# Window attention, then top-1 MoE: column groups for small last blocks, experts 1 and 2 swapped, one pass of 160 columns, held products at the end, maxima scaled by ScalarE

## The chip, the cores and the metric

The kernel runs on one core of one Trainium2 chip. The metric is the device time of one execution in microseconds (us), and less is better. TensorE (PE) does the matrix products, VectorE (DVE), ScalarE (ACT) and GpSimd (POOL) the elementwise work, and SyncE (SP) issues most of the transfers. The views of the profile show PE's weight loads as an engine of their own, PEld.

## The reference

```python
# q, k, v: 8 x 8 x 576 x 64; window of 64 keys up to the query's own
scores = where(mask, (q @ k.T) / 8, -1e9)
scores = scores - max(scores)
attn = exp(scores); attn /= sum(attn) + 1e-9
x = (attn @ v).transpose(0, 2, 1, 3).reshape(4608, 512)
logits = x @ w_gate                      # 8 experts
e = argmax(logits); gate = softmax(logits)[e]
for each expert: out[mask] = gate * (relu(x[mask] @ w1[e]) @ w2[e])   # 512 -> 1024 -> 512
```

## The kernel before

**Attention** works in 36 steps of 128 rows, software-pipelined: in step `i` PE makes the scores of tile `i` (L419), DVE folds the two halves of the window (L430), reduces the maxima (`largest`, L436) and multiplies them by 1/8 (L438); in the next step ACT makes the exponentials with these as bias (`exps`, L446); PE transposes them (L451), ACT copies them out (`tsb`, L455), POOL masks them (`pm`, L462), and a step later PE multiplies with the values (`x_b`, L476) and DVE divides (`xrow`, L486). Rows are transposed back (L493, copied by ACT at L500), and every fourth step PE makes the logits in four groups of 32 columns of its array (L537). Names: `s_b`, `t_b`, `m_b`, `x_b`, `e_b` are PSUM banks.

**Experts.** Rows are sorted into blocks of 128 per expert. The first two blocks of experts 0 to 3 run early, as four passes of 256 rows, the first of them woven into the last attention steps. Meanwhile `plan` (POOL and DVE, small operations on 8 counts, one part after each piece of an early pass) assigns the other blocks to slots of a fixed list: SLOTS (blocks, columns, how many) and then narrow slots of 2 blocks and 256 columns. `chain` then runs eleven passes, numbered 0 to 10, in the order that ORDER gives; their widths are 256, 320, 416, 416, 512, 512, 384, 256, 256, 256, 256 columns. All of them run whatever the data, and more narrow ones only if the count of narrow slots that `plan` finds exceeds ALWAYS (5); none did here.

**One pass** has 8 iterations `j`, one for each 128 of the 1024 hidden columns. The weights of two iterations come as one transfer of 1 MB into `raw` (three buffers). `split` makes two reduced-precision halves of them, `whi` on ACT (L253) and `wlo` on DVE (L250), so that each full product is three fast ones. In an iteration PE makes the first layer, 12 matmuls over the pass's width (L323, L327); ACT and DVE make `hh` and `hl` from it (L333, L334); then `flush` makes the second layer of the iteration before: for each block of 128 rows three matmuls of 512 columns (L295). A last block of 32 or 64 rows costs the same three. After the last iteration ACT scales a block by its gate (`ys`, L282) and POOL scatters its rows (L283).

**Loads.** All `raw` transfers and the transposes of the next pass's rows are issued by SP in program order. The next pass's first three are issued in iterations 3, 4 and 6 (`ready`), the last one in the pass's own iteration 2; a buffer comes free when `whi` and `wlo` of both its slices are made.

Of the kernel before, what the change touches and what calls it, by code (L numbers as in the profile page):

```python
# [72 lines left out]
SPACE = (159, 168)  # L73
# [9 lines left out]
for _n, _w in (("fold", W), ("ident", P), ("mask", 2 * P), ("tri", P), ("desc", E), ("ebase", E), ("elow", 2 * E),  # L83
               ("st0", E), ("eid", E), ("tcol", NT), ("row", P), ("first", 2 * EARLY), ("pcol", 1), ("scol", 1), ("ucol", 1),
               ("kind", 5), ("at", 5)):
    CO[_n] = (_off, _w)
    _off += _w
# [4 lines left out]
def constants():  # L92
# [13 lines left out]
    put("desc", E - e)  # L106
# [16 lines left out]
    is_ = kind[:, None] == np.arange(5)[None]  # L123
    put("kind", is_)
    last = is_[:, 0] | is_[:, 2]
    put("at", np.stack([last, -4 * is_[:, 0] - 3 * is_[:, 2], ~last, 3 * (is_[:, 1] | is_[:, 4]), 4 * is_[:, 4]], 1))
# [4 lines left out]
def window_attention_then_top1_moe(ctx: ExitStack, tc: tile.TileContext, qkv, wall, wg, cst, out):  # L131
# [47 lines left out]
    starts = const.tile([P, 5 * E], F32, name="starts")  # L179
# [29 lines left out]
    class Weights:  # L209


        def __init__(self, ev, spread=0, far=False):
            self.far = far
# [26 lines left out]
        def split_(self, pieces=None, lows=None):  # L240
# [23 lines left out]
            if self.far and r and self.loaded < min(jj + 3, NJ // 2):  # L264
                self.load()
            return hi, lo
# [4 lines left out]
    late = []  # L271

    def flush(final=False):
# [3 lines left out]
        (hh, hl), yp, (hi, lo), j, w, last = late.pop()  # L277
        def finish(u):
# [3 lines left out]
            nc.scalar.activation(out=ys[0:n], in_=yp[u][0:n], func=AF.Copy, scale=gate)  # L282
# [8 lines left out]
        for u, y in enumerate(yp):  # L291
            n = min(P, w - u * P)
            us = slice(u * P, u * P + n)
            for m, (x, ww) in enumerate(((hh, hi), (hh, lo), (hl, hi))):
                nc.tensor.matmul(y[0:n], lhsT=x[:, us], rhs=ww[:, C:], start=(j == 0 and m == 0),  # L295
                                 stop=(j == NJ - 1 and m == 2))
            if final:
                finish(u)
            if u + 1 < len(yp):
                yield  # L300
        if last is not None and not final:
            for u in range(len(yp)):
                finish(u)
        yield

    def expert(xt, idx, gates, wts, following=None, w=2 * P):
# [6 lines left out]
        for j in range(NJ):  # L313
# [4 lines left out]
            hi, lo = cur  # L318
# [14 lines left out]
            nc.scalar.activation(out=hh[:, 0:w], in_=hp[:, 0:w], func=AF.Relu)  # L333
            nc.vector.scalar_tensor_tensor(out=hl[:, 0:w], in0=hp[:, 0:w], scalar=0.0, in1=hh[:, 0:w],  # L334
                                           op0=ALU.max, op1=ALU.subtract)
            yield
            yield from flush()
            if yp is None:
                yp = [bank("yp") for u in range(nu)]
            late.append(((hh, hl), yp, cur, j, w, (idx, gates) if j == NJ - 1 else None))  # L340
            cur = nxt
            yield j
# [42 lines left out]
    for k in range(5):  # L385
# [46 lines left out]
    def largest(n):  # L432
# [285 lines left out]
    def plan():  # L718
        cm = rt.tile([P, 5, E], F32, name="cm", bufs=1)
# [10 lines left out]
        ev = of("ev2", two("ev", half, 2.0, ALU.is_ge), two("even", odd, 0.5, ALU.is_lt), ALU.mult)  # L730
        of("ev3", ev, two("few", spare, float(P - LQ), ALU.is_ge), ALU.mult, want2[:, 0])
# [7 lines left out]
        p3 = of("p3", odds, cm[:, 2], ALU.subtract)  # L739
# [4 lines left out]
        stt("c3", running("c3r", p3)[:, 0], float(SLOTS[3][2]), p3, ALU.is_le, ALU.mult, out=cm[:, 3])  # L744
        yield
        l1 = of("l3", two("third", cm[:, 3], -3.0, ALU.mult), l1, ALU.add)
        p1 = two("p1", l1, 4.0, ALU.is_ge)
# [13 lines left out]
        mine = rt.tile([P, 5, E], F32, name="sums_", bufs=1)  # L761
        nc.vector.tensor_tensor(out=mine, in0=sums, in1=kind.unsqueeze(2).to_broadcast([P, 5, E]), op=ALU.mult)
# [106 lines left out]
    def ready(i, j):  # L869
# [6 lines left out]
        if j == 3:  # L876
            open_weights(i)
        if j in (4, 6):
            wts[i].load()

    def open_weights(i):
        wts[i] = Weights(expert_of(passes[i][0]), far=True)
# [229 lines left out]
```

## Time and profile before

| what | value |
|---|---|
| median of 3 runs | 620.65 us (619.53 to 623.07) |
| the profiled execution's own time | 618.47 us |
| its span, first to last instruction | 616.7 us (1.8 us lie around it) |
| mean granted TensorE clock | 0.998 |
| attention, up to the last step that only it fills | about 0 to 153 us |
| early passes | about 153 to 260 us |
| the eleven passes | 260.3 to about 609 us, then the last scatters |

The first six lines of such a profile say how busy each engine is in the span; the timeline gives single instructions, with the idle time before them and what ended it in brackets. Where PE runs without brackets, the distance between the starts of two matmuls is what the first of them costs.

### The profile page before, as it was taken

How to read it: one execution, taken by the hardware profiler on the slowest of the kernel's cores; microseconds unless marked ns; L12 is line 12 of the kernel's file. 1: busy time of each engine (PE TensorE's matmuls, PEld its weight loads, DVE VectorE, ACT ScalarE, POOL GpSimd, SP SyncE). 2: the span in 40 equal slices, each digit the busy share in tenths (PEclk: the TensorE clock that was granted, in tenths of full speed). 3: DMA queues.
4: the chain of work that ended last, by engine and by line, in shares of the span. 5: the costliest groups of instructions: out<-in, count | busy, mean ns of one | idle time of the engine just before them, and what ended most of it. 6: DMA issues, size and time to landing. Idle time of an engine off the chain costs nothing.

```text
span 616.7 us, 15804 instructions
## 1 busy us (share of the span) xinstructions
PE 582.6 (94%) x6467; PEld 500.6 (81%) x6467; DVE 378.4 (61%) x673; ACT 357.9 (58%) x735; POOL 205.9 (33%) x212
## 2 busy tenths in 40 slices
PE   8699989798999999999999999999999999999995
PEld 4587878676878889987888888888888899999994
DVE  3676778987776996657564554444444535667651
ACT  4577766777535665657664546446426446667752
POOL 3656657567447115042223050040120311232011
PEclk9999999999999999999999999999999999999999
DMA  8978878864586686886949377294282473886731
GB/s 288 383 255 271 291 246 280 291 233 134 195 307 208 232 262 166 314 249 205 274 154 276 125 132 265 69 231 152 83 266 84 117 271 102 298 260 216 256 140 36
DMA packets 71747, 132.83 MB, mean 215 GB/s; under 512 B 42604, under 2 KB 43756, under 8 KB 64240
## 3 DMA queue, kind: packets, MB, share of 16 engines
q1 hardware_dynamic: 65392, 112.84, 56.9%
q0 software_dynamic: 6272, 18.88, 10.0%
q8 instruction: 52, 0.85, 0.6%
q14 instruction: 31, 0.25, 0.1%
HBM read 104.44 MB, written 19.40 MB: 201 GB/s over the span
## 4 chain that ended last, share of the span: by engine, by line
PE 69%; issue 11%; DVE 7%; POOL 7%; ACT 3%; DMA 1%; POOLq 0%; SPq 0%; DVEq 0%; ACTq 0%
PE e_b L323 18%; PE e_b L295 12%; PE e_b L327 9%; PE x_b L295 6%; PE t_b L295 5%; PE x_b L476 5%; PE m_b L295 4%; PE s_b L419 3%; POOL pm L462 3%; PE m_b L493 2%; PE m_b L537 2%; DVE wlo L250 2%; POOL out L283 1%; DMA raw<-wall 1%; PE t_b L451 1%
## 5 line engine op out<-in xcount | busy, mean ns | idle before, releaser
L250 DVE TENSOR_TENSOR wlo<-raw,whi 128x1024 fp32r<-128x1024 f32 (+1 forms) x126 | 149.1, 1183 | 62.4 <-ACT whi L253 62.2
L333 ACT ACTIVATE hh<-e_b 128x256 fp32r<-128x256 f32 (+4 forms) x120 | 53.1, 442 | 177.0 <-PE e_b L327 176.9
L283 POOL DMA_INDIRECT out<-ys,idx_sb x32 | 38.5, 1202 | 267.8 <-ACT ys L282 262.3
L253 ACT CAST whi<-raw 128x1024 fp32r<-128x1024 f32 (+1 forms) x121 | 121.4, 1004 | 4.0 <-DMA raw<-wall 4.0
L334 DVE SCALAR_TENSOR_TENSOR hl<-e_b,hh 128x256 fp32r<-128x256 f32 (+4 forms) x120 | 59.0, 492 | 91.4 <-ACT hh L333 91.3
L323 PE MATMUL e_b<-xh,whi 128*128 128x256 f32 (+4 forms) x352 | 108.1, 323 | 1.4 <-ACT whi L253 1.4
L462 POOL TENSOR_TENSOR pm<-tsb,cs 128x512 f32<-128x512 f32 x72 | 90.0, 1271 | 54.5 <-ACT tsb L455 48.3
L323 PE MATMUL e_b<-xl,whi 128*128 128x256 f32 (+4 forms) x352 | 108.0, 323 | 0.0
L323 PEld LDWEIGHTS e_b<-xh,whi 128*128 128x128 f32 x352 | 66.4, 189 | 9.8 <-ACT whi L253 2.3
L323 PEld LDWEIGHTS e_b<-xl,whi 128*128 128x128 f32 x352 | 66.4, 189 | 5.8
L327 PE MATMUL e_b<-xh,wlo 128*128 128x256 f32 (+4 forms) x352 | 70.7, 322 | 0.1
L446 ACT ACTIVATE pf<-s_b,mxs 128x64 f32<-128x64 f32 x288 | 63.0, 338 | 10.5 <-DVE mxs L438 8.4
L476 PE MATMUL x_b<-ring,pm 64*64 64x65 f32 x2176 | 47.2, 222 | 14.7 <-issue 8.4
L327 PEld LDWEIGHTS e_b<-xh,wlo 128*128 128x128 f32 x352 | 56.4, 188 | 3.5 <-DVE wlo L250 0.5
L476 PEld LDWEIGHTS x_b<-ring,pm 64*64 64x64 f32 x2176 | 41.7, 134 | 20.5 <-issue 13.5
L295 PE MATMUL e_b<-whi,hl 128*128 128x512 f32 x144 | 56.4, 392 | 0.7 <-DVE hl L334 0.7
L295 PE MATMUL e_b<-whi,hh 128*128 128x512 f32 x144 | 56.5, 392 | 0.0
L295 PE MATMUL e_b<-wlo,hh 128*128 128x512 f32 x144 | 56.5, 392 | 0.0
L848 ACT COPY joined<-halves 128x1024 uint16<-128x1024 uint16 x36 | 47.8, 1351 | 0.0
L191 POOL DMA_INDIRECT rows<-xs,idx_sb x32 | 37.5, 1173 | 26.9 <-issue 24.5
L500 ACT COPY xT<-m_b 128x512 f32<-128x512 f32 x36 | 21.2, 588 | 43.0 <-PE m_b L493 42.9
L419 PE MATMUL s_b<-ring 64*64 64x128 f32 x1024 | 41.6, 278 | 0.8 <-issue 0.8
(193 smaller groups left out, 1016.3 us busy)
## 6 DMA issues: line engine op xcount, KB each, us to landing
raw<-wall SPq DMA_DIRECT2D x58, 1024.0 KB, 7.3
ring<-qkv SPq DMA_DIRECT2D x66, 386.0 KB, 4.9
xs<-xrow SPq DMA_DIRECT2D x36, 256.0 KB, 3.9
raw<-wall SPq DMA_DIRECT2D x8, 256.0 KB, 5.4
rows<-xs SPq DMA_DIRECT2D x2, 1024.0 KB, 9.9
ring<-qkv SPq DMA_DIRECT2D x4, 256.0 KB, 5.5
halves<-planes SPq DMA_TRANSPOSE x36, 4.9
ring<-qkv SPq DMA_DIRECT2D x4, 130.0 KB, 5.2
```

The source lines that it names most:

```text
L250: nc.vector.tensor_tensor(out=lo[:, s], in0=raw[:, s], in1=hi[:, s], op=ALU.subtract)
L253: nc.scalar.copy(out=hi[:, s], in_=raw[:, s])
L295: nc.tensor.matmul(y[0:n], lhsT=x[:, us], rhs=ww[:, C:], start=(j == 0 and m == 0), stop=(j == NJ - 1 and m == 2))
L323: nc.tensor.matmul(hp[:, 0:w], lhsT=hi[:, ks], rhs=x[:, kk, 0:w], start=(kk == 0 and x is xh), stop=False)
L327: nc.tensor.matmul(hp[:, 0:w], lhsT=lo[:, kk * P:(kk + 1) * P], rhs=xh[:, kk, 0:w], start=False, stop=(kk == 3))
L333: nc.scalar.activation(out=hh[:, 0:w], in_=hp[:, 0:w], func=AF.Relu)
L334: nc.vector.scalar_tensor_tensor(out=hl[:, 0:w], in0=hp[:, 0:w], scalar=0.0, in1=hh[:, 0:w], op0=ALU.max, op1=ALU.subtract)
L419: nc.tensor.matmul(sp[cols, a, g], lhsT=q_r[rows, r, g], rhs=k_r[rows, r - 1:r + 1, g], start=True, stop=True)
L446: nc.scalar.activation(out=pf[:, g, a], in_=sp[:, a, g, 0], func=AF.Exp, bias=mx[:, h:h + 1], scale=SCALE)
L462: nc.gpsimd.tensor_tensor(out=pm[i], in0=t.rearrange("p (g q) -> p g q", g=NG), op=ALU.mult, in1=cc("mask")[:, i * P:(i + 1) * P].unsqueez ...
L476: nc.tensor.matmul(x_b[cols, a, g * V1:(g + 1) * V1], lhsT=pm[i][rows, g, cols], rhs=v_r[rows, c % RING - i, g], start=(i == 0), stop=(i = ...
L848: nc.scalar.copy(out=x.rearrange("p k t -> p (k t)").bitcast(U16).rearrange("p (t s) -> p s t", s=2), in_=halves.pop(key).rearrange("p (s ...
```

## The change

- `flush`: where the width leaves a last block of 32 or 64 rows (`few`), its `hf` is kept in plain float32 and multiplied with `raw` itself. The 512 output columns are split into 4 groups of 128 (32 rows) or 2 groups of 256 (64 rows), each on columns of the array of its own. ACT makes `hf` beside `hh`; the scaling of the block is split over ACT and DVE.
- Since PE then reads `raw`, a buffer of such a pass (`held`) comes free only after the products of its second slice. The pass loads its last weights at the end of iteration 2, and the next pass's first two are opened at the end of iterations 4 and 6, its third one pass later in iteration 0.
- SLOTS gets a slot of 2 blocks and 160 columns, and ALWAYS falls from 5 to 4: pass 7 is 160 columns wide. Experts 1 and 2 change places (PERM), so that other counts meet the early passes; `plan` gets the rows of a fifth kind.
- In a chain's last pass the products of the second block of iterations 5 and 6 are held back by one `flush` each, so that the first block is done earlier; the last scaling is halved over ACT and DVE.
- The maxima are multiplied by 1/8 on ACT, ahead of the exponentials, and no longer on DVE.
- SPACE, two unused tiles, get smaller.

```diff
-SLOTS = ((4, 416, 2), (4, 512, 2), (3, 320, 1), (3, 384, 1))
+SLOTS = ((4, 416, 2), (4, 512, 2), (3, 320, 1), (3, 384, 1), (2, 160, 1))
+PERM = (0, 2, 1, 3, 4, 5, 6, 7)
-ALWAYS = 5
-TAIL = [5, 6, 8, 12, 18]
-ORDER = (6, 4, 0, 1, 2, 3, 5, 7, 8, 9, 10)
+ALWAYS = 4
+TAIL = [4, 5, 7, 11, 17]
+ORDER = (7, 4, 0, 1, 2, 3, 5, 6, 8, 9, 10)
...
-            if self.far and r and self.loaded < min(jj + 3, NJ // 2):
+            if self.far and not self.held and r and self.loaded < min(jj + 3, NJ // 2):
...
+    def few(w):
+        n = w % P
+        return n if n in (LQ, W) else 0
...
+            k = P // n if hf is not None and u + 1 == len(yp) else 1
+            if parted and k == 1:
+                at = C // 2
+                nc.scalar.activation(out=ys[0:n, 0:at], in_=yp[u][0:n, 0:at], func=AF.Copy, scale=gate)
+                nc.vector.tensor_scalar(out=ys[0:n, at:], in0=yp[u][0:n, at:], scalar1=gate, scalar2=None, op0=ALU.mult)
...
+            if hf is not None and u + 1 == len(yp):
+                k = P // n
+                for g in range(k):
+                    nc.tensor.matmul(y[g * n:(g + 1) * n, 0:C // k], lhsT=hf[:, 0:n],
+                                     rhs=raw[:, C + g * C // k:C + (g + 1) * C // k], start=(j == 0), stop=(j == NJ - 1))
+            else:
+                for m, (x, ww) in enumerate(((hh, hi), (hh, lo), (hl, hi))):
...
+        if ending and NJ - 3 <= j < NJ - 1 and len(yp) == 2:
+            product(0)
+            yield
+            while held:
+                held.pop(0)()
+            held.append(lambda: product(1))
...
+            if wts.held and j % 2 == 0 and wts.loaded < j // 2 + 3:
+                wts.load()
...
-        mxs[n] = wk.tile([P, H], F32, name="mxs")
-        nc.vector.tensor_scalar(out=mxs[n], in0=mx, scalar1=SCALE, scalar2=None, op0=ALU.mult)
+        mxs[n] = mx
...
-        sp, mx = sp_of(n), mxs.pop(n)
+        sp, mx = sp_of(n), wk.tile([P, H], F32, name="mxs")
+        nc.scalar.mul(out=mx, in_=mxs.pop(n), mul=SCALE)
...
-        if j == 3:
+        held = i > 0 and few(widths[i - 1]) > 0
+        if j == 3 + held:
             open_weights(i)
-        if j in (4, 6):
+        if j in ((6,) if held else (4, 6)):
             wts[i].load()
```

Three places show how instructions move. The first is PE's row of work in pass 2 (416 columns), from the second layer's third block to the next first layer; `t_b` and `m_b` are the banks of blocks 3 and 4. Before:

```order
L295 MATMUL t_b<-whi,hh 128x512
L295 MATMUL t_b<-wlo,hh 128x512
L295 MATMUL t_b<-whi,hl 128x512
L295 MATMUL m_b<-whi,hh 32x512
L295 MATMUL m_b<-wlo,hh 32x512
L295 MATMUL m_b<-whi,hl 32x512
L323 MATMUL e_b_3375<-xh,whi 128x416
```

And now:

```order
L321 MATMUL t_b<-whi,hh 128x512
L321 MATMUL t_b<-wlo,hh 128x512
L321 MATMUL t_b<-whi,hl 128x512
L317 MATMUL m_b<-raw,hf 32x128 x4
L366 MATMUL e_b_3376<-xh,whi 128x416
```

Three matmuls of 512 columns became four of 128, one in each column group. The second place is PE in pass 7, one iteration's end and the next one's start. Before:

```order
L327 MATMUL e_b_3376<-xh,wlo 128x256 x4
L295 MATMUL x_b<-whi,hh 128x512
L295 MATMUL x_b<-wlo,hh 128x512
L295 MATMUL x_b<-whi,hl 128x512
L295 MATMUL e_b_3334<-whi,hh 128x512
L295 MATMUL e_b_3334<-wlo,hh 128x512
L295 MATMUL e_b_3334<-whi,hl 128x512
L323 MATMUL e_b_3375<-xh,whi 128x256
```

And now:

```order
L370 MATMUL e_b_3377<-xh,wlo 128x160 x4
L321 MATMUL x_b<-whi,hh 128x512
L321 MATMUL x_b<-wlo,hh 128x512
L321 MATMUL x_b<-whi,hl 128x512
L317 MATMUL e_b_3333<-raw,hf 32x128 x4
L366 MATMUL e_b_3376<-xh,whi 128x160
```

The first layer has as many matmuls as before, each over 160 columns. The third place is POOL in `plan`, up to the second half of `want`, for which DVE's scan `c02r` waits. Before:

```order
L695 TENSOR_SCALAR ev<-halfr 128x8
L695 TENSOR_SCALAR even<-odd 128x8
L702 TENSOR_TENSOR ev_3891<-ev,even 128x8
L695 TENSOR_SCALAR few<-spare 128x8
L702 TENSOR_TENSOR want_3842<-ev_3891,few 128x8
L695 TENSOR_SCALAR less<-spare 128x8
L702 TENSOR_TENSOR want_3842<-odds,less 128x8
```

And now:

```order
L745 TENSOR_SCALAR even<-odd 128x8
L745 TENSOR_SCALAR few<-spare 128x8
L752 TENSOR_TENSOR ev_3892<-even,few 128x8
L745 TENSOR_SCALAR ev<-halfr 128x8
L752 TENSOR_TENSOR want_3843<-ev_3892,ev 128x8
L745 TENSOR_SCALAR one_3897<-halfr 128x8
L752 TENSOR_TENSOR pair<-ev_3892,one_3897 128x8
L745 TENSOR_SCALAR less<-spare 128x8
L752 TENSOR_TENSOR want_3843<-odds,less 128x8
```

Two small operations (`one_`, `pair`) stand ahead of the one that releases DVE.

## Rows read from the trace of the kernel before

**Rows 1.** The page: each engine's busy us, share of the span, instructions.
```profile
PE 582.6 (94%) x6467; PEld 500.6 (81%) x6467; DVE 378.4 (61%) x673; ACT 357.9 (58%) x735; POOL 205.9 (33%) x212
```

**Rows 2.** Timeline of PE, pass 7 (256 columns): start us, us, what.
```profile
521.11 0.28 PE L323 MATMUL e_b<-xh,whi 128*128 128x256 f32 x1
...
522.06 0.64 PE L327 MATMUL e_b<-xh,wlo 128*128 128x256 f32 x4
522.53 0.39 PE L295 MATMUL x_b<-whi,hh 128*128 128x512 f32 x1
...
523.91 0.28 PE L323 MATMUL e_b<-xh,whi 128*128 128x256 f32 x1
```

**Rows 3.** Timeline of PE, pass 3 (416 columns).
```profile
359.83 0.35 PE L323 MATMUL e_b<-xh,whi 128*128 128x416 f32 x1
...
364.86 0.35 PE L323 MATMUL e_b<-xh,whi 128*128 128x416 f32 x1
```

**Rows 4.** Maxima on DVE, an ACT copy of their shape, attention's waits (total us, times, longest).
```profile
L438 DVE TENSOR_SCALAR mxs<-s_b 128x8 f32<-128x8 f32 x36 | 6.0, 166 | 1.2
...
L393 ACT COPY base<-cs x1: 275/275/275, 34.1 to 34.1; 128x8 f32<-128x8 f32 x1
...
PEld x_b L476 <- POOL pm L462: 6.2, 11, 1.4
...
PE x_b L476 <- DVE xrow L486: 3.1, 6, 1.2
```

**Rows 5.** Timeline of POOL, DVE and PE around one of `plan`'s scans.
```profile
190.10 0.23 POOL L695 TENSOR_SCALAR few<-spare 128x8 f32<-128x8 f32 x1
...
190.59 0.23 POOL L695 TENSOR_SCALAR less<-spare 128x8 f32<-128x8 f32 x1
...
191.14 0.19 DVE L712 TENSOR_TENSOR_SCAN c02r<-starts,want 128x16 f32<-128x16 f32 x1 [3.67 <-POOL want L702]
...
191.99 0.50 PE L295 MATMUL x_b<-whi,hl 128*128 128x512 f32 x1 [1.09 <-DVE hl L334]
```

**Rows 6.** Timeline of PE where the logits stand inside an early pass's first layer.
```profile
167.58 0.28 PE L323 MATMUL e_b<-xel,whi 128*128 128x256 f32 x1
167.79 1.08 PE L537 MATMUL m_b<-xT,wg_sb 128*32 128x128 f32 x32
168.80 0.73 PE L327 MATMUL e_b<-xeh,wlo 128*128 128x256 f32 x4
169.37 0.40 PE L295 MATMUL e_b<-whi,hh 128*128 128x512 f32 x1
```

**Rows 7.** Timeline of PE in one attention step: four transposes of 128 columns, then four more.
```profile
62.09 0.65 PE L493 MATMUL m_b<-cs,xrow 128*128 128x128 f32 x4
62.58 0.60 PE L451 MATMUL t_b<-cs,pf 128*128 128x128 f32 x4
```

**Rows 8.** Timeline of PE, pass 1 (320 columns).
```profile
299.36 0.40 PE L295 MATMUL x_b<-whi,hh 128*64 128x512 f32 x1
...
300.05 0.31 PE L323 MATMUL e_b<-xh,whi 128*128 128x320 f32 x1
```

**Rows 9.** Groups by line and shape, weight loads: count, busy us, mean ns, idle before.
```profile
L323 PEld LDWEIGHTS e_b<-xh,whi 128*128 128x128 f32 x352 | 66.4, 189 | 9.8 <-ACT whi L253 2.3
...
L295 PEld LDWEIGHTS m_b<-wlo,hh 128*32 128x32 f32 x8 | 0.9, 108 | 0.9
```

**Rows 10.** The weights' tile `raw`, issue to landing; and its casts by line and shape.
```profile
DMA to landing us min/median/max: 4.7/6.5/10.5
...
L253 ACT CAST whi<-raw 128x1024 fp32r<-128x1024 f32 x113 | 118.1, 1046 | 4.0 <-DMA raw<-wall 4.0
```

**Rows 11.** Timeline of the end: PE's last matmul, and POOL's last two scatters.
```profile
609.04 0.39 PE L295 MATMUL e_b<-whi,hl 128*128 128x512 f32 x1
...
609.75 0.97 POOL L283 DMA_INDIRECT out<-ys,idx_sb  x1 [18.70 <-ACT ys L282]
611.02 0.97 POOL L283 DMA_INDIRECT out<-ys,idx_sb  x1 [0.30 <-issue]
```

More of the change, by code (lines that the diff above doesn't have):

```diff
@@ L84 @@
                ("st0", E), ("eid", E), ("tcol", NT), ("row", P), ("first", 2 * EARLY), ("pcol", 1), ("scol", 1), ("ucol", 1),
[L85 removed]
+               ("kind", KINDS), ("at", 5)):
     CO[_n] = (_off, _w)
@@ L122, in constants @@
     put("ucol", ucol[:, None])
-    is_ = kind[:, None] == np.arange(5)[None]
+    is_ = kind[:, None] == np.arange(KINDS)[None]
     put("kind", is_)
-    last = is_[:, 0] | is_[:, 2]
-    put("at", np.stack([last, -4 * is_[:, 0] - 3 * is_[:, 2], ~last, 3 * (is_[:, 1] | is_[:, 4]), 4 * is_[:, 4]], 1))
+    last = is_[:, 0] | is_[:, 2] | is_[:, 4]
+    put("at", np.stack([last, -4 * is_[:, 0] - 3 * is_[:, 2] - 2 * is_[:, 4], ~last, 3 * (is_[:, 1] | is_[:, 5]),
+                        4 * is_[:, 5]], 1))
     return c
@@ L289, in finish, with product @@
             outs.append(ins)
-        for u, y in enumerate(yp):
-            n = min(P, w - u * P)
+        def product(u):
+            y, n = yp[u], min(P, w - u * P)
             us = slice(u * P, u * P + n)
[L294 to L301, printed above, removed]
+            if hf is not None and u + 1 == len(yp):
+                k = P // n
+                for g in range(k):
+                    nc.tensor.matmul(y[g * n:(g + 1) * n, 0:C // k], lhsT=hf[:, 0:n],
+                                     rhs=raw[:, C + g * C // k:C + (g + 1) * C // k], start=(j == 0), stop=(j == NJ - 1))
+            else:
+                for m, (x, ww) in enumerate(((hh, hi), (hh, lo), (hl, hi))):
+                    nc.tensor.matmul(y[0:n], lhsT=x[:, us], rhs=ww[:, C:], start=(j == 0 and m == 0),
+                                     stop=(j == NJ - 1 and m == 2))
+        if final:
+            product(0)
+            finish(0)
+            while held:
+                held.pop(0)()
+            for u in range(1, len(yp)):
+                product(u)
+                finish(u, u + 1 == len(yp))
+            return
+        if ending and NJ - 3 <= j < NJ - 1 and len(yp) == 2:
+            product(0)
+            yield
+            while held:
+                held.pop(0)()
+            held.append(lambda: product(1))
+        else:
+            for u in range(len(yp)):
+                product(u)
+                if u + 1 < len(yp):
+                    yield
+        if last is not None:
             for u in range(len(yp)):
@@ L384, in window_attention_then_top1_moe @@
     nc.vector.memset(starts, 1.0)
-    for k in range(5):
+    for k in range(KINDS):
         nc.vector.memset(starts[:, k * E:k * E + 1], 0.0)
@@ L729, in plan @@
         yield
-        ev = of("ev2", two("ev", half, 2.0, ALU.is_ge), two("even", odd, 0.5, ALU.is_lt), ALU.mult)
-        of("ev3", ev, two("few", spare, float(P - LQ), ALU.is_ge), ALU.mult, want2[:, 0])
+        ev = of("ev2", two("even", odd, 0.5, ALU.is_lt), two("few", spare, float(P - LQ), ALU.is_ge), ALU.mult)
+        of("ev3", ev, two("ev", half, 2.0, ALU.is_ge), ALU.mult, want2[:, 0])
+        pair = of("pair", ev, two("one2", half, 1.0, ALU.is_ge), ALU.mult)
         of("p2", odds, two("less", spare, float(W), ALU.is_ge), ALU.mult, want2[:, 1])
@@ L743, in plan @@
             yield
-        stt("c3", running("c3r", p3)[:, 0], float(SLOTS[3][2]), p3, ALU.is_le, ALU.mult, out=cm[:, 3])
+        ends = running("c34r", more2.rearrange("p k e -> p (k e)"), 2)
+        stt("c3", ends[:, 0], float(SLOTS[3][2]), more2[:, 0], ALU.is_le, ALU.mult, out=cm[:, 3])
+        stt("c4", ends[:, 1], float(SLOTS[4][2]), more2[:, 1], ALU.is_le, ALU.mult, out=cm[:, 4])
         yield
         l1 = of("l3", two("third", cm[:, 3], -3.0, ALU.mult), l1, ALU.add)
+        l1 = of("l3b", two("pairs", cm[:, 4], -2.0, ALU.mult), l1, ALU.add)
         p1 = two("p1", l1, 4.0, ALU.is_ge)
@@ L875, in ready @@
         prepare(j, late_rows[i % 2], len(passes[i]), i, columns_of)
-        if j == 3:
+        held = i > 0 and few(widths[i - 1]) > 0
+        if j == 3 + held:
             open_weights(i)
-        if j in (4, 6):
+        if j in ((6,) if held else (4, 6)):
             wts[i].load()
     def open_weights(i):
-        wts[i] = Weights(expert_of(passes[i][0]), far=True)
+        wts[i] = Weights(expert_of(passes[i][0]), far=True, held=few(widths[i]) > 0)
     def each(f, n):
```

60 lines of the change are left out of this document (37 added, 23 removed).

## The prediction

> **What bounds the kernel now.** I first read the page: PE is busy in 94% of the span, no other engine in more than 61% [rows 1]. That is an average, so I then read PE's timeline stage by stage, looking for idle time in brackets. From 260 us to the end there is none but a little at the start of the chain: the next first layer starts when the last matmul has been fed, and the distance of two starts is the price. In pass 7 twelve first-layer matmuls of 256 columns take 522.53 − 521.11 = 1.42 us, 0.118 each, and six of the second layer 523.91 − 522.53 = 1.38, 0.230 each; an iteration is 2.80 [rows 2]. At 416 columns an iteration is 364.86 − 359.83 = 5.03; less twelve times 0.230 that leaves 2.27, or 0.189 for each first-layer matmul [rows 3]. Shorter work on PE is therefore worth its full length in the eleven passes. In attention and the early passes others hold PE up too: the product with the values waits 3.1 us for `xrow` and its weight loads 6.2 us for `pm` [rows 4], and in `plan` PE stalls 1.09 us behind DVE, which waited 3.67 us for POOL's `want` [rows 5]. So the chain's parts are costed on PE, and the others by what waits for them.
>
> **Column groups, 416 columns (passes 2 and 3).** Per iteration three matmuls of 512 columns, 3 × 0.230 = 0.69, become four float32 products of 128 columns, which the trace counts as eight. The nearest row is the logits, which use the same four groups and float32: 32 records, eight rounds of four, between two stretches of fast matmuls [rows 6]. From the last L323 before them to the first L327 behind them is 168.80 − 167.58 = 1.22. Of this 0.12 is the usual distance of a first-layer matmul; on the other side the four L327 then take 169.37 − 168.80 = 0.57 instead of 0.47, so 0.10 is added: 1.20 for eight rounds. How it divides isn't shown. Four float32 transposes over 128 columns are 0.49 us apart, 0.12 each [rows 7]; I take 0.11 for a round of the same length with four groups side by side, which leaves 1.20 − 0.88 = 0.32 for going in and out. Two rounds are then 0.22 + 0.32 = 0.54, a gain of 0.15 in each of 16 iterations: **−2.4 us**. Bounds: if all 1.20 belongs to the rounds, two are 0.30 and the gain is 0.39 × 16 = 6.2; if the burst is mostly entry and exit, 0.69 is reached and nothing is gained.
>
> The Trainium skill, "TensorEngine Tiling (Array Packing)", section "Key Properties", says that a change of tiling mode drains TensorE; by its "Theoretical Speedup" table up to four times is to be had at 32 columns. The 1.20 for eight rounds agrees with the drain, and does not show its size for two rounds. By the table alone the sum would end near 608, by the drain near 616.
>
> **320 columns (pass 1).** Three matmuls, 300.05 − 299.36 = 0.69 [rows 8], become two groups of 256 columns: two rounds of twice the length, 0.44, the same 0.32, and 0.03 for 64 instead of 32 weight columns: 0.79. **+0.8 us** over eight iterations; were groups of two not to run side by side, 0.44 more each, +4.3; without the 0.32, −1.8.
>
> **Pass 7, 160 columns.** Six second-layer matmuls become three and a burst: −0.15 as above. The first layer keeps its twelve matmuls, at 160 columns each. By the columns (0.189/416 = 0.45 ns) one would cost 0.073. But each has a 128-column weight load of its own. Loads of 128 and 32 columns take 189 and 108 ns [rows 9], 0.84 ns a column, so an estimate of 0.108 for what one of 128 occupies; and the transposes, with weights of 128 columns too, are spaced by 0.12 over only 128 columns [rows 7]. I take 0.113, between 0.108 and 0.118: 12 × 0.005 = 0.06. The iteration falls to 2.80 − 0.15 − 0.06 = 2.59, eight of them **−1.7 us**. Bounds: 0.073 gives 12 × 0.045 × 8 = 4.3 for the first layer alone, −5.5 in all; no gain there and 0.15 in the second layer gives −1.2.
>
> The Trainium skill, "TensorE: Matmul & The Clock Gate", section "LDWEIGHTS (loading the stationary operand)", prices a load by its columns, which makes 107 ns for 128: it speaks against a gain here, and [rows 9] agree. The same page's "Back-to-back issue gap" gives some 81 ns sustained at 128 columns: 160 columns would then lie near the column price, which is the rival R1. The transposes of [rows 7] speak for the first, though their operand isn't the same.
>
> **Loads.** In the four held passes a buffer is free later, so the load that pass 7 opens at the end of iteration 2 is needed at the third iteration after it, 3 × 2.59 = 7.8 us later. A load lands 4.7, 6.5 or 10.5 us after its issue (least, median, most), and the cast is 1.05 [rows 10]: 7.6 at the median, hidden by 0.2, uncovered by 3.9 at the most. Passes 2 and 3 have 15 us for three iterations [rows 3], pass 1 by the same prices 3 × (12 × 0.145 + 9 × 0.23 + 0.10) = 11.7, and I expect no stall there. I take +0.4 for pass 7 and its successor; bounds 0 and +7.3 (R3 below). If a stall stands there, `whi` is late next, then the first layer.
>
> **`plan`.** Two more POOL operations stand ahead of `want`. Two of that size are 190.59 − 190.10 = 0.49 [rows 5], and DVE already waited there, with `hl` and so PE's second layer behind the waiting scan; all 0.49 reaches PE. Two more for the fifth kind stand ahead of a later scan, and DVE's operations over six kinds are wider: +0.6 by estimate, of the same row. **+1.1 us**, bounds 0.5 and 2.5 (all four operations at twice their length, and half a microsecond on DVE).
>
> **The end.** PE's last matmul starts at 609.04, the first of the last two scatters at 609.75, 0.97 long, and the second at 611.02 [rows 11]: its `ys` was late by 0.30. With the second block's products held back, the first block is done three matmuls (0.69) earlier, and the last `ys` is halved over two engines. Then the last scatter waits for PE's end and its own scaling, some 0.3 shorter, instead of for the other scatter. **−0.7 us**, bounds 0 and −1.0. PE's work stays the same in sum.
>
> **Maxima.** 36 DVE operations of 0.166 go, 36 ACT operations of about 0.275 come [rows 4], in front of the exponentials. On DVE 6.0 us are removed and on ACT 9.9 us added, in a stage where neither bounds every step. What is next in line behind ACT are the exponentials, `tsb`, `pm` and the value product, whose loads already wait 6.2 us for `pm`; what is relieved is `xrow`, with 3.1. A tenth of a microsecond a step, on some steps: **+0.3**, bounds −3.0 (all the waits for `xrow` go) and +3.0 (0.275 in the 11 steps that wait for `pm`). Work hidden there costs nothing only while PE has that step's other matmuls to do.
>
> **The sum.** −2.4 + 0.8 − 1.7 + 0.4 + 1.1 − 0.7 + 0.3 = −2.2. The profiled execution took 618.47, 2.2 under the median of 620.65. The same difference on the median gives **618.4 us**, −0.36%. From no change 0.5%, 3.1 us, can be told: faster is below 617.5, slower above 623.8.
>
> **Rivals.**
> - *R1, 160 columns cost by the columns.* Then the first layer is 0.073 each and pass 7 gives 5.5 instead of 1.7; but iterations of 2.1 us leave 6.3 for loads that want 7.6, and of that some 1.3 us is given back in two places. Net −1.2 to −3.8 more: 615.9. For it: at 416 and 256 the price is proportional to the columns [rows 2, 3]. Against: [rows 7, 9]. Chance 0.17.
> - *R2, bursts at full speed.* Entry and exit cost nothing for a short burst: 0.22 for 0.69 in 24 iterations at 32 rows (416 twice, 160 once) and 0.44 at 320: −0.47 × 24 − 0.25 × 8 = −13.3 instead of −2.8, so about 608. Against: 1.20 for eight rounds [rows 6]. Chance 0.05.
> - *R3, late loads: the slower side.* If the loads around pass 7 land at 10.5 us instead of 6.5 [rows 10], `whi` of its last slice is late by 10.5 + 1.05 + 0.1 − 7.8 = 3.9, and that of pass 8's second load, issued at the end of iteration 6 and needed 8.2 later, by 3.4: +7.3 instead of +0.4, 625.3. It decides when both land later than some 9.5. For it: held buffers take away the slack that all other passes of 256 have. Against: the median, and that few other transfers run there. Chance 0.08.
> - *R4, ACT's maxima on the path.* All of +3: 621.1. For it: 6.2 us of waits for `pm`. Against: ACT is idle in 42% of the span. Chance 0.10.
> - *R5, DVE's relief shortens attention*, −2 instead of +0.3: 616.1. For it: 3.1 us of waits for `xrow`. Chance 0.10.
> - *R6, it doesn't do what it says*: with four narrow slots a further pass becomes needed, 8 × 2.80 = 22.4, some 641. The counts speak against it. Chance 0.01.
>
> The forecast has the remaining 0.49, with a range of its own from 615.5 to 621. **How the numbers follow.** Faster by over 0.5%: R2 (0.05), R5 (0.08), R1 (0.12) and the lower third of the forecast (0.17), 0.42. Slower: R3 (0.07), R6, and the upper ends of R4 and the forecast (0.04), 0.12. Same: 0.46. From 613.0 to 622.5 leaves out R2, R6, most of R3 and what R1 and R4 have at their ends, near 0.18.
>
> **What would show it.** In passes 2 and 3 the distance from the last fast matmul ahead of the `raw` products to the next first layer should be 0.54 more than one matmul's, in pass 1 0.79; iterations of 4.88 and 3.91. In pass 7 the first layer should be spaced by 0.113 and iterations be 2.59. ACT's cast of `raw` should wait for a transfer, if anywhere, late in pass 7 and early in pass 8. The scan behind `want` should wait 0.5 longer. The first of the last scatters should stand some 0.7 nearer to PE's end. The step in which I trust least is the division of 1.20 into rounds and overhead, since 24 iterations hang on it; after it the 0.113.

## The result and the profile after

The changed kernel took 624.32 us (median of 20 runs), the kernel before 620.13 in 20 runs beside it: a ratio of 1.0062, 95% interval 1.0041 to 1.0082. The ratio leaves out the two slowest executions, 630.24 and 797.94 (granted clock 0.655), the median does not. The kernel is slower, where 618.4 and a range of 613.0 to 622.5 had been given. The profiled execution took 623.76, with a span of 622.0, against 618.47 and 616.7. Where its 5.3 us came from is read from the starts of the passes' first matmuls:

| stretch | before | after | difference |
|---|---|---|---|
| up to the first early pass | 153.94 | 152.90 | −1.0 |
| four early passes, with the plan | 106.40 | 107.50 | +1.1 |
| pass 0 | 25.10 | 25.20 | +0.1 |
| pass 1 (320 columns) | 29.93 | 30.47 | +0.5 |
| passes 2 and 3 (416) | 79.62 | 77.61 | −2.0 |
| passes 4 to 6 | 122.65 | 122.63 | 0.0 |
| pass 7 (256, now 160) | 23.08 | 27.26 | +4.2 |
| pass 8 (256) | 22.40 | 24.57 | +2.2 |
| pass 9 (256) | 22.40 | 22.40 | 0.0 |
| pass 10 and the end | 31.17 | 31.42 | +0.2 |

Passes 7 and 8 took 51.83 instead of 45.48, 6.4 more; the other stretches together took 1.1 less. PE's timeline there (start us, us, what, in brackets the idle time and what ended it), against [rows 2]:

```profile
527.39 0.34 PE L366 MATMUL e_b<-xh,whi 128*128 128x160 f32 x1
527.57 0.28 PE L366 MATMUL e_b<-xl,whi 128*128 128x160 f32 x1
527.68 0.27 PE L366 MATMUL e_b<-xh,whi 128*128 128x160 f32 x1
...
529.71 0.43 PE L317 MATMUL e_b<-raw,hf 128*32 128x128 f32 x8
530.07 0.34 PE L366 MATMUL e_b<-xh,whi 128*128 128x160 f32 x1
...
532.30 0.42 PE L317 MATMUL e_b<-raw,hf 128*32 128x128 f32 x8
534.61 0.34 PE L366 MATMUL e_b<-xh,whi 128*128 128x160 f32 x1 [1.88 <-ACT whi L256]
...
538.86 0.50 PE L366 MATMUL e_b<-xh,whi 128*128 128x160 f32 x1
```

In iteration 4 (527.39 to 530.07) the first layer is spaced by 0.11 and hardly anything waits (2.68, where iterations 2 and 3 take 2.59). Iteration 6 begins 1.88 us late, for `whi`. From then on the same iteration is 4.25 long (534.61 to 538.86). The same stretch by windows (PE, PEld, DVE, ACT, POOL busy, granted clock, DMA share, GB/s) shows why:

```profile
530.00:534.60 4.60, 2.73 (x31) 1.98 (x23) 0.17 (x2) 1.78 (x3) 0.00 (x0) 1.00 0.97 374
534.60:535.90 1.30, 1.16 (x9) 1.00 (x9) 1.30 (x2) 1.30 (x3) 0.00 (x0) 1.00 0.14 57
535.90:546.20 10.30, 10.30 (x50) 8.04 (x51) 5.49 (x8) 4.59 (x10) 0.00 (x0) 0.50 0.38 118
546.20:560.00 13.80, 13.65 (x93) 11.87 (x93) 8.99 (x14) 7.85 (x12) 6.29 (x4) 1.00 0.82 236
```

1.3 us after PE has gone on, the granted clock falls to 0.50, 1.2 of 2.4 GHz, and stays there for 10.3 us. ACT's timeline says for what `whi` waited, and shows something else ahead of it:

```profile
521.45 0.28 ACT L378 ACTIVATE hh<-e_b 128x128 fp32r<-128x128 f32 x1
...
525.75 0.28 ACT L378 ACTIVATE hh<-e_b 128x128 fp32r<-128x128 f32 x1 [3.00 <-PE e_b L317]
...
533.51 1.04 ACT L256 CAST whi<-raw 128x1024 fp32r<-128x1024 f32 x1 [2.82 <-DMA raw<-wall]
```

The cast waits 2.82 us for the last load of the pass. And the `hh` of iteration 2 stands at 525.75, though the first layer that it reads had ended at 523.78 by PE's records: PE's signal reached ACT 2 us late. SP, which waits for PE to have read the held buffer, got its signal late too (what the queue waited for, us in total, times, longest, and the load that followed):

```profile
SPq L238 <- PE e_b L370: 5.3, 1, 5.3
...
527.39 0.35 SPq L238 DMA_DIRECT2D raw<-wall  x1
```

The products that free the buffer end at 524.87; the load is issued at 527.39, 11.1 us into the pass. It lands 6.1 later, an ordinary time by [rows 10].

The other places. Pass 3, where [rows 3] show 5.03 an iteration:

```profile
359.53 0.46 PE L366 MATMUL e_b<-xh,whi 128*128 128x416 f32 x1
...
363.74 0.39 PE L321 MATMUL e_b<-whi,hl 128*128 128x512 f32 x1
364.05 0.42 PE L317 MATMUL t_b<-raw,hf 128*32 128x128 f32 x8
364.41 0.46 PE L366 MATMUL e_b<-xh,whi 128*128 128x416 f32 x1
```

That is 4.88. Pass 1 [rows 8] has 300.40 and 304.32 for two starts, 3.92. In the plan, against [rows 5], on POOL, DVE and PE:

```profile
189.56 0.23 POOL L745 TENSOR_SCALAR one<-halfr 128x8 f32<-128x8 f32 x1
189.88 0.20 POOL L752 TENSOR_TENSOR pair<-ev,one 128x8 f32<-128x8 f32 x1
...
190.59 0.19 DVE L762 TENSOR_TENSOR_SCAN c02r<-starts,want 128x16 f32<-128x16 f32 x1 [4.14 <-POOL want L752]
...
191.45 0.50 PE L321 MATMUL x_b<-whi,hl 128*128 128x512 f32 x1 [1.57 <-DVE hl L382]
```

DVE's wait grew from 3.67 to 4.14, PE's from 1.09 to 1.57. At the end, against [rows 11]:

```profile
614.09 0.39 PE L321 MATMUL e_b<-whi,hl 128*128 128x512 f32 x1
614.12 0.97 POOL L303 DMA_INDIRECT out<-ys,idx_sb  x1 [18.03 <-ACT ys L300]
614.51 0.47 ACT L294 ACTIVATE ys<-e_b,gate_sb 128x256 f32<-128x256 f32 x1 [0.67 <-PE e_b L321]
615.02 0.48 DVE L295 TENSOR_SCALAR ys<-e_b,gate_sb 128x256 f32<-128x256 f32 x1 [3.08 <-ACT ys L294]
616.10 0.97 POOL L303 DMA_INDIRECT out<-ys,idx_sb  x1 [1.01 <-DVE ys L295]
```

The first scatter is earlier, as meant. But DVE's half of the last scaling waits for ACT's, so that the two take 0.99 in a row where one of full length took 0.69, and the last scatter stands 2.01 behind the start of PE's last matmul, 1.98 before.

### The profile page after: what moved, and what is told of

It reads as the page before. It is cut to its first block, busy times and chain, and to the rows that moved or that the text cites. A ratio compares the mean times of both kernels' runs of the same rounds, so it can differ in the third digit from the quotient of the medians.

```text
span 622.0 us, 16099 instructions
## 1 busy us (share of the span) xinstructions
PE 585.3 (94%) x6595; PEld 494.0 (79%) x6595; DVE 376.7 (61%) x650; ACT 363.6 (58%) x803; POOL 213.7 (34%) x217
## 4 chain that ended last, share of the span: by engine, by line
PE 64%; issue 12%; POOL 12%; DVE 6%; ACT 3%; DMA 2%; POOLq 0%; DVEq 0%; ACTq 0%
PE e_b L366 18%; PE e_b L321 11%; PE e_b L370 9%; POOL pm L512 7%; PE x_b L321 5%; PE t_b L321 4%; PE m_b L321 4%; PE x_b L526 3%; DMA raw<-wall 2%; PE s_b L469 2%; DVE wlo L253 2%; PE m_b L543 1%; POOL out L303 1%; ACT pf L496 1%; PE m_b L587 1%
## 5 line engine op out<-in xcount | busy, mean ns | idle before, releaser
L378 ACT ACTIVATE hh<-e_b 128x256 fp32r<-128x256 f32 (+3 forms) x120 | 51.4, 428 | 180.9 <-PE e_b L370 170.9
L303 POOL DMA_INDIRECT out<-ys,idx_sb x32 | 44.4, 1387 | 266.2 <-ACT ys L300 259.5
L366 PE MATMUL e_b<-xh,whi 128*128 128x256 f32 (+5 forms) x352 | 112.5, 335 | 2.7 <-ACT whi L256 2.7
L382 DVE SCALAR_TENSOR_TENSOR hl<-e_b,hh 128x256 fp32r<-128x256 f32 (+3 forms) x120 | 56.9, 475 | 88.8 <-ACT hh L378 61.5
L366 PE MATMUL e_b<-xl,whi 128*128 128x256 f32 (+5 forms) x352 | 108.8, 325 | 0.0
L370 PE MATMUL e_b<-xh,wlo 128*128 128x256 f32 (+5 forms) x352 | 72.1, 327 | 0.4 <-DVE wlo L253 0.2
L526 PE MATMUL x_b<-ring,pm 64*64 64x65 f32 x2176 | 48.7, 222 | 14.9 <-issue 9.0
L321 PE MATMUL e_b<-whi,hh 128*128 128x512 f32 x136 | 53.5, 393 | 0.6 <-ACT hh L378 0.6
L321 PE MATMUL e_b<-whi,hl 128*128 128x512 f32 x136 | 53.4, 392 | 0.7 <-DVE hl L382 0.7
L321 PE MATMUL e_b<-wlo,hh 128*128 128x512 f32 x136 | 53.4, 392 | 0.0
```

What stands on the lines that cost most here:

```text
L303: ins = nc.gpsimd.indirect_dma_start(out=out, out_offset=bass.IndirectOffsetOnAxis(ap=ix, axis=0), in_=ys[0:n], in_offset=None, bounds_che ...
L366: nc.tensor.matmul(hp[:, 0:w], lhsT=hi[:, ks], rhs=x[:, kk, 0:w], start=(kk == 0 and x is xh), stop=False)
L370: nc.tensor.matmul(hp[:, 0:w], lhsT=lo[:, kk * P:(kk + 1) * P], rhs=xh[:, kk, 0:w], start=False, stop=(kk == 3))
L378: nc.scalar.activation(out=hh[:, 0:r], in_=hp[:, 0:r], func=AF.Relu)
L382: nc.vector.scalar_tensor_tensor(out=hl[:, 0:r], in0=hp[:, 0:r], scalar=0.0, in1=hh[:, 0:r], op0=ALU.max, op1=ALU.subtract)
L526: nc.tensor.matmul(x_b[cols, a, g * V1:(g + 1) * V1], lhsT=pm[i][rows, g, cols], rhs=v_r[rows, c % RING - i, g], start=(i == 0), stop=(i = ...
```

## The experiments

Theory A: holding pass 7's buffers makes its last load late as a rule; PE stalls and then runs at half the clock. Theory B: the late signals come from elsewhere, such as POOL's gathers. Theory C: ACT has too much to do. Theory D came with the second group: the load is late only where signals come late. The ratios are to the kernel before, run beside each group on the same chip. Which chip a group ran on was left to chance, and it turned out to matter.

**First group, one chip.** Four kernels, each the changed one with one part undone.

```diff
# no_hold7
-        return n if n in (LQ, W) else 0
+        return n if n in (LQ, W) and w > 2 * P else 0
# wide7
-SLOTS = (... (2, 160, 1))
+SLOTS = (... (2, 256, 1))
# mxs_dve
-        mxs[n] = mx
+        mxs[n] = wk.tile([P, H], F32, name="mxs")
+        nc.vector.tensor_scalar(out=mxs[n], in0=mx, scalar1=SCALE, scalar2=None, op0=ALU.mult)
...
-        sp, mx = sp_of(n), wk.tile([P, H], F32, name="mxs")
-        nc.scalar.mul(out=mx, in_=mxs.pop(n), mul=SCALE)
+        sp, mx = sp_of(n), mxs.pop(n)
# no_groups
-        return n if n in (LQ, W) else 0
+        return 0
```

> Pass 7 stays 160 columns wide, but its last block of 32 rows is made with the three fast matmuls again, so its weight buffers aren't held. Theory A (the buffers held in pass 7 make its last load late; PE stalls, and then runs at half the granted clock): no stall in pass 7 and no fall of the clock; iterations of 12 x 0.113 + 6 x 0.23 = 2.73 us, passes 7 and 8 together 45.0 us instead of 51.8; 0.3% faster than before. Theory B (the late signals from PE that stand in that stretch come from somewhere else, such as the gathers on POOL): the stall stays, 0.6% slower than before.

> The slot of 160 columns is 256 wide (zero-weight rows more, the same result), so that pass 7 has neither held buffers nor short iterations; all else as in the changed kernel. Theory A: passes 7 and 8 take 45.5 us as before, and what is left is attention -1.0, plan +1.1, pass 1 +0.5, passes 2 and 3 -2.0: 0.2% faster than before. Theory B: 0.5% slower or more.

> The maxima are scaled on DVE again, all else as in the changed kernel. Theory A: the chain keeps its stall in pass 7, and attention gives its 1.0 us back: 0.8% slower than before. Theory C (ACT is burdened by 36 more operations, and this is where the time went): the kernel gains, 0.3% slower than before or less. If the stall in pass 7 hangs on where POOL's and SP's work falls, this run shows it too, since only the time of its start differs.

> No column groups: every last block is made with the three fast matmuls, and no buffer is held; 160 columns, the order of experts, the end and the maxima stay. Theory A: no stall; pass 1 back to 29.9, passes 2 and 3 to 79.6, passes 7 and 8 together 45.0: 0.1% faster than before, and 0.2% slower than the kernel without the hold in pass 7 alone. Theory B: about 0.8% slower than before.

| kernel | ratio | 95% interval | passes 7 and 8 |
|---|---|---|---|
| no_hold7 | 0.9953 | 0.9925 to 0.9981 | 44.90 |
| wide7 | 0.9976 | 0.9947 to 1.0005 | 45.48 |
| mxs_dve | 0.9993 | 0.9966 to 1.0020 | 44.23 |
| no_groups | 0.9977 | 0.9945 to 1.0010 | 44.90 |

Without the hold the stall is gone, as A said, but it is gone with maxima on DVE too, which A and C had not said and in which the hold stands. Either the maxima matter to a pass 360 us later, or the stall isn't there on this chip. The later groups and the record of signals (last section) speak for the second; the changed kernel itself was not run on this chip. The intervals allow no finer reading: the kernels without the hold differ among themselves by less than they are wide.

**Second group, another chip.** The changed kernel again; its gathers moved; the buffer of the last load freed one iteration later; and a version with the costs mended that had shown so far.

```diff
# gather_late (chain)
-                if j == 2 and i + 2 < last:
+                if j == (5 if i == 7 else 2) and i + 2 < last:
# later (flush; with four buffers for hf)
-        if ending and NJ - 3 <= j < NJ - 1 and len(yp) == 2:
+        if (ending and NJ - 3 <= j < NJ - 1 or w == 160 and j < NJ - 1) and len(yp) == 2:
...
+            while held and w == 160:
+                held.pop(0)()
# mended
-        return n if n in (LQ, W) else 0
+        return n if n == LQ and w > 2 * P else 0
...
-        pair = of("pair", ev, two("one2", half, 1.0, ALU.is_ge), ALU.mult)
         of("p2", odds, two("less", spare, float(W), ALU.is_ge), ALU.mult, want2[:, 1])
+        pair = of("pair", ev, two("one2", half, 1.0, ALU.is_ge), ALU.mult)
...
-                finish(u, u + 1 == len(yp))
+                finish(u)
```

> The changed kernel itself once more, on one chip with the others here. Theory A (the hold in pass 7 makes its last load late as a rule): a stall in pass 7 and a fall of the granted clock behind it in the profile, 0.6% slower than before. Theory D (the load is late only where PE's signals happen to come late, which they did in that one execution and not in that of the kernel with maxima on DVE): no stall here, passes 7 and 8 near 44.2 us as with maxima on DVE, and no more than 0.1% slower than before.

> In pass 7 POOL gathers the rows of a later pass behind iteration 5 and no longer behind iteration 2; all else as in the changed kernel. In the profile of the changed kernel PE's signals around 523.8 to 527.3 us came up to 2 us late while POOL issued these gathers. Theory B (the gathers make them late): the last load of pass 7 is issued at the end of iteration 2, no stall, passes 7 and 8 about 44.2 us, 0.2% faster than before. If the gathers have no part in it: as the changed kernel run beside it, within 0.2%.

> In pass 7 the products that read the held weights are made one iteration later (as the end's held products are), so that the buffer of its last load comes free 2.6 us later; the same work otherwise. Theory A: the load is issued at iteration 4's start at the earliest, lands 4.5 to 6 us later, and PE stalls 1 to 3 us in iterations 5 and 6 in every execution, with the clock at half behind it: passes 7 and 8 at 50 to 54 us, 0.7% slower than before or more. If a load late by 2.6 us costs only its own stall: passes 7 and 8 at 45 to 47 us, 0.1 to 0.3% slower.

> Column groups for 32 rows at 416 columns alone (none at 320, none at 160, so no hold in pass 7), the two new operations of the plan behind those that DVE waits for, and the last scaling whole on ACT; all else as in the changed kernel. By the pieces measured so far: attention -1.0, plan +0.6, passes 2 and 3 -2.0, pass 7 -0.6, the end -0.5 us: -3.5 us, 0.6% faster than before, and 0.1 to 0.2% faster than without the hold alone.

The changed kernel measured 0.9990 (0.9966 to 1.0013) here, not 1.0062. Its profile has no stall before the last iteration; on SP and ACT, in the same places as above (this pass began at 519.27, 2.95 later):

```profile
SPq L238 <- PE e_b L317: 3.0, 1, 3.0
...
528.00 0.35 SPq L238 DMA_DIRECT2D raw<-wall  x1
...
526.77 0.28 ACT L378 ACTIVATE hh<-e_b 128x128 fp32r<-128x128 f32 x1 [1.06 <-PE e_b L370]
...
534.04 1.05 ACT L256 CAST whi<-raw 128x1024 fp32r<-128x1024 f32 x1 [0.50 <-DMA raw<-wall]
```

The load is issued 8.7 us into the pass, at the end of iteration 2, lands in 6.0, and `whi` is just in time; passes 7 and 8 take 44.54. So A falls as a rule, and D stands. `later` puts the lateness back by construction; its load on SP, and PE's iteration 6 (this pass began at 517.42):

```profile
528.49 0.35 SPq L238 DMA_DIRECT2D raw<-wall  x1
...
535.82 0.34 PE L368 MATMUL e_b<-xh,whi 128*128 128x160 f32 x1 [2.33 <-ACT whi L256]
```

The load is issued at 11.1, as in the result's profile, and passes 7 and 8 take 50.29, with the clock at half again (6.8 us); 1.0095 (1.0059 to 1.0131). The same 2.4 us, however they come about, cost some 6. `gather_late` measured 0.9979 (0.9953 to 1.0004) and says nothing: its gathers stood where they had, 7.6 us into the pass, since POOL had nothing else to do between the two places in the program, and no signal was late. `mended` measured 0.9950 (0.9928 to 0.9971).

**Third group, a third chip.** The changed kernel and the mended one again, and both with the held products of pass 7 made in their own iteration, which frees the buffer 2.6 us sooner.

```diff
# sooner, mended_sooner (expert; flush leaves them out)
+            if w == P + LQ:
+                for g in range(P // n):
+                    nc.tensor.matmul(yp[1][g * n:(g + 1) * n, 0:C // (P // n)], lhsT=hf[:, 0:n], ...)
             late.append(((hh, hl, hf), yp, cur, j, w, ...))
```

> The changed kernel a third time, on whichever chip comes. Theory A (late as a rule): 0.6% slower than before, with the stall. Theory D (late only where PE's signals come late): SP's wait ahead of the last load of pass 7 tells which it is; 2.9 us as in two executions goes with passes 7 and 8 at 44.5 us and a time within 0.3% of before, 5.3 us goes with 50 us or more and 0.6% slower.

> In pass 7 the products that read the held weights are made in their own iteration, behind the second layer of the iteration before, so that the buffer of the last load comes free 2.6 us sooner; the same work otherwise. If the slack of that load is what decides (A and D): issued near 5.9 us into the pass instead of 8.7, landed at 12, and the casts no longer wait for it; passes 7 and 8 at 43.4 to 44.0 us, faster than the changed kernel beside it by 0.1%, or by 0.8% where that one stalls. If PE waits for the product's operand instead, iterations of 2.7 to 2.9 us and nothing gained.

> The mended kernel (groups for 32 rows alone, plan in the other order, last scaling whole) with column groups at 160 columns too, and their products in their own iteration. Pass 7 at 2.59 us an iteration instead of 2.73, so 1.1 us less than mended beside it: 0.6 to 0.7% faster than before. If pass 7 or 8 stalls in spite of the earlier load, no faster than mended.

> The mended kernel once more, beside the others of this call: 0.5% faster than before, whatever happens to the changed kernel here, since no buffer of pass 7 is held in it.

Here the changed kernel was at 1.0063 (1.0040 to 1.0086), with a wait of 5.4 on SP and 50.95 us in passes 7 and 8. `mended` was at 0.9975 (0.9954 to 0.9996) on the same chip. Its profile has late signals too; ACT in pass 7, next to POOL:

```profile
525.98 0.30 ACT L378 ACTIVATE hh<-e_b 128x160 fp32r<-128x160 f32 x1 [3.22 <-PE e_b L321]
...
522.52 1.19 POOL L303 DMA_INDIRECT out<-ys,idx_sb  x1 [0.30 <-issue]
524.01 1.13 POOL L194 DMA_INDIRECT rows<-xs,idx_sb  x1 [0.30 <-issue]
525.45 1.01 POOL L194 DMA_INDIRECT rows<-xs,idx_sb  x1 [0.31 <-issue]
```

It loses nothing by them: passes 7 and 8 take 44.91, because `hh` is wanted an iteration later and no load waits for PE. `sooner` was the worst, 1.0144 (1.0109 to 1.0179), and `mended_sooner` was at 1.0019 (0.9987 to 1.0050). The load of `sooner` was issued at 8.2, not 5.9, and PE now waited itself for what the late signal releases:

```profile
526.24 0.40 PE L321 MATMUL x_b<-whi,hl 128*128 128x512 f32 x1
528.50 0.43 PE L392 MATMUL e_b<-raw,hf 128*32 128x128 f32 x8 [1.86 <-ACT hf L383]
```

Its clock is at 0.63 on average over the next 23 us, and pass 7 takes 31.75. What was meant to give slack took away the iteration that had absorbed a late signal.

**Last runs, in four groups, each on a chip as it came.** They were to tell whether the gathers in pass 7 make the signals late. `after_fourth` and `after_fifth` are the changed kernel, `gather_late_again` and `gather_late_third` the kernel above beside it, whose gathers stand where they had, so these two tell no more than the changed kernel does. `gather_wait` and `gather_wait4` hold the gathers back on POOL itself:

```diff
+                if i == 7 and j == 6:        # 4 in gather_wait4
+                    w = hw.tile([P, 8], F32, name="wait", bufs=1)
+                    nc.gpsimd.tensor_scalar(out=w, in0=late[-1][0][2][:, 0:8], scalar1=1.0, scalar2=None, op0=ALU.mult)
-                if j == 2 and i + 2 < last:
+                if j == (6 if i == 7 else 2) and i + 2 < last:        # 4 in gather_wait4
```

> The changed kernel a fourth time, to stand beside the run with later gathers. Where signals come late under POOL's gathers: SP's wait ahead of the last load of pass 7 5.3 us, passes 7 and 8 at 50 us or more, 0.6% slower than before. Where they don't: wait 2.9 us, 44.5 us, within 0.3% of before.

> Pass 7's gathers behind its iteration 5, as before. If the gathers make the signals late and nothing else does: where the changed kernel beside it has the wait of 5.3 us, this one has 2.9 us, passes 7 and 8 at 44.5 us, 0.8% faster than the changed kernel. If something else makes them late: a wait of 5.3 us here too, and the same time as the changed kernel. On a chip where no signal comes late the two are alike and this says nothing.

> The changed kernel beside the run with later gathers, on another chip. Where signals come late under POOL's gathers: SP's wait ahead of the last load of pass 7 5.3 us, passes 7 and 8 at 50 us or more, 0.6% slower than before. Where they don't: 2.9 us, 44.5 us, 0.1 to 0.4% faster than before.

> Pass 7's gathers behind its iteration 5. If they alone make the signals late: a wait of 2.9 us and 44.5 us on every chip, and 0.8% faster than the changed kernel where that one stalls. If something else does: the same wait and time as the changed kernel beside it.

> In pass 7 POOL waits for a tile of iteration 6, 17 us into the pass, before it gathers; the gathers otherwise stand 7.6 us into it. On a chip where signals come late elsewhere in the profile (during POOL's transfers of passes 0 to 4): if the gathers make them late, SP's wait ahead of the last load is 2.9 us, no stall in pass 7 before iteration 6, passes 7 and 8 at 44 to 46 us and a time of 0.2% faster than before; if they don't, the wait is 5.3 us, passes 7 and 8 at 50 us or more, 0.5% slower. On a chip where no signal comes late: 44.5 us, and it says nothing.

> As the run before, but POOL waits for a tile of iteration 4, 13 us into the pass. On a chip where signals come late elsewhere in the profile: if the gathers make them late, SP's wait ahead of the last load of pass 7 is 2.9 us and pass 7 takes 21.4 to 22 us; if they don't, 5.3 us and 26 us or more. On a chip where no signal comes late: 2.9 us, passes 7 and 8 at 44.5 us, and it says nothing on the gathers.

| kernel | ratio | 95% interval | SP's wait | passes 7 and 8 |
|---|---|---|---|---|
| after_fourth | 0.9963 | 0.9937 to 0.9988 | 3.0 | 45.35 |
| gather_late_again, same chip | 0.9964 | 0.9933 to 0.9996 | 3.0 | 44.25 |
| after_fifth | 1.0049 | 1.0017 to 1.0080 | 5.4 | 50.91 |
| gather_late_third, same chip | 1.0023 | 0.9993 to 1.0054 | 5.4 | 51.31 |
| gather_wait | 1.0010 | 0.9978 to 1.0043 | 2.9 | 49.87 |
| gather_wait4 | 0.9933 | 0.9904 to 0.9962 | 2.9 | 44.03 |

`gather_wait` fell on the chip of the second group and `gather_wait4` on that of `after_fourth`; neither chip showed late signals either time, so the question stays open. The first of them shows only that gathers held back to 19.8 us into pass 7 make pass 8 stall (28.44 us).

## Why the prediction was wrong

**The step that failed** is the term "I take +0.4 for pass 7 and its successor". It rested on the load being issued at the end of iteration 2, with 0.2 us to spare at the median landing. Where that holds, the step holds too: in `after_again` the load is issued at 8.7 and `whi` is ready some 0.4 us before iteration 6. Passes 7 and 8 then gained 0.9 us in `after_again` and 0.1 in `after_fourth`, where the sum had −1.7 + 0.4. In the result's profile, and in two of the four repeats, the issue came 2.4 us later, because PE's signal did. The five executions of the changed kernel divide cleanly: with a wait of 5.3 to 5.4 on SP passes 7 and 8 take 50.9 to 51.8 us and the ratio is 1.0049 to 1.0063; with 3.0 they take 44.5 to 45.4 and it is 0.9963 to 0.9990. These are one profile of each run. Within the result's own run, three of the 20 executions have a granted clock of 0.996 or 0.997, which leaves room for some 5 us at half in all and so not for a fall of 10; they took 620.6 to 621.8, about the time of the kernel before. So the fall is not in every execution on such a chip.

**Rival R3** had the place and the sign, and a chance of 0.08. It had the wrong cause: it let the load land late (10.5 us), and the landings were 5.9 to 6.5. And it priced the delay by itself; that its +7.3 is the cost measured here is chance. In the result's profile PE's own stall is 1.9 us, and passes 7 and 8 cost 7.3 more than in `after_again`; most of the rest is the half clock behind it, for which the sum had no term, as no stall in the chain stood in the profile of before. That the delay is enough is shown by `later`. That the hold is needed is what `mended` says beside the changed kernel on the third chip; it differs in three more places, none of them in pass 7. `no_hold7`, which differs in the hold alone, was run only where nothing stalled with the hold either.

**416 columns**: 0.54 for the burst and 4.88 an iteration were forecast and 4.88 measured; −2.0 over the two passes instead of −2.4, since an iteration fell by 0.14 (5.02 to 4.88), 15 of the 16 bursts stand in these passes, and pass 2's first iteration carries one of pass 1's, +0.1. Of the 0.54, 0.44 stand ahead of the next first layer, 364.41 − 363.74 less one matmul, and 0.10 in that layer's first matmul, which takes 0.30 instead of 0.20. **320**: 3.91 forecast, 3.92 measured, +0.5 instead of +0.8. The division of 1.20 into rounds and overhead, in which I trusted least, held. R2 is out. In the prediction's comparison of "near 608" with "near 616" the first goes by the median and the second by the profiled execution; on the median the second is its own 618.4.

**160 columns**: 2.59 forecast and 2.59 measured; the first layer is spaced by 0.11, so R1 is out. The Trainium skill, "TensorE: Matmul & The Clock Gate", section "LDWEIGHTS (loading the stationary operand)", prices a load of 128 columns at 107 ns, and the spacing of 0.11 agrees, though a load's own record is 189 ns long [rows 9]; the 81 ns that its "Back-to-back issue gap" gives for 128 columns don't fit this stream of 160.

**The plan**: +1.1 forecast, +1.1 measured in the early passes, 1.0 of it in the second (25.13 before, 26.16 now). In nine other profiles the granted clock also falls for 3.4 us in the first early pass, which then takes 33.4 to 33.5 instead of 32.1, so the second is the one to compare. `mended`, with the two operations behind those that DVE waits for, has 0.5 us less in the second early pass (25.70 against 26.16).

**The end**: −0.7 forecast, 0.0 measured; the term was lost where I let the halves run side by side. The reading that the last `ys` had been late by 0.30 was wrong as well: ACT had both ready at 610.16 before, and [rows 11] put the 0.30 down to `issue`, as POOL's lines of the third group do between scatters in a row. `mended` scales on ACT alone: 607.69 for PE's last matmul, 609.39 for the last scatter, 1.70 instead of 2.01.

**Maxima**: +0.3 forecast. On ACT they took 0.183 each, 6.6 us in all, not the 0.275 and 9.9 of the one copy that I went by. The 1.0 us gained in the profile can't be put down to them: in 18 profiles with maxima on ACT the first early pass starts between 150.0 and 158.0, in `mxs_dve` at 152.7, before at 153.9. Their effect is smaller than that scatter and stays open.

**The sum** without late signals was −2.2; the two repeats without them gave ratios of 0.9990 and 0.9963, −0.6 and −2.3 us. With late signals, passes 7 and 8 take 5.6 to 7.3 us more.

**A version that beats both** is `mended`: 0.9950 and 0.9975 on two chips, one of each kind, without a load that waits for PE in pass 7. `gather_wait4` at 0.9933 was run on one chip only, one of the harmless kind.

## What to carry to other kernels

When an edit makes a buffer live longer, work out the slack of its next load from issue to use, with the release of the buffer at its latest and not only the landing, and call a slack of a few tenths none. Price a stall in a stretch without gaps by what it does to the clock, not by its own length: 1.9 us cost 7 here. And before a change of half a per cent is believed either way, run it on more than one chip, and look in a profile of each for the wait on which it hangs.

## What the runs showed of the hardware

Signals between engines can come late: here they do in the result's profile (whose chip is not on record) and in all profiles of two chips, and hardly ever in those of three others. I took the first recorded update from an instruction's end on as its signal. In the eleven passes of `after_third`, PE ended 58 signalling matmuls while POOL was issuing a gather or scatter (or up to 1 us behind). For 12 of them the update stands 0.2 to 5.9 us behind the end, and at nine of these, 0.2 to 3.0 us late, an engine that had been idle goes on just then. None of the 136 others is late. By the same count DVE had 13 late ones of 78 and ACT 12 of 86 in such periods, and none outside them. The seven profiles of the result, the third and the fifth chip are all like this (PE 10 to 14); the 13 others have two at most, of all three engines.

In these seven profiles some updates are not on record at all: in `after_third` 607 for DVE's 625 signals, 541 for ACT's 554, 435 for PE's 440, while the others have at least as many updates on record as signals. So an update that stands late may be that of a later signal, and the counts are rough; the engines that go on late, and SP's load, are not. PE's matmuls themselves keep their distance meanwhile. That POOL's transfers cause it is not shown, only that nothing came late without them. Nor is it shown whether the recording has a part in it, since every execution here was recorded.

In each of the seven profiles in which PE stalled for 1.7 to 2.4 us in pass 7 (the six such profiles with the hold, and `later`), the granted clock fell to half between 0.8 us before PE went on and 2.3 us after, and stayed there for 6.8 to 17.1 us. That is at least one whole iteration, 4.73 us long instead of 2.59, in which PE worked without a pause. Ahead of the stall it had been 1.00 in the chain. A wait of 0.7 us in pass 8 of `sooner` and of `mended_sooner` was followed by no fall.
